# Loading both query weights in two pieces, of 16 and of 112 partitions

## The chip, the cores and the metric

The kernel runs on one core of a Trainium2 chip. The metric is the device time of one execution in microseconds. The core has a matrix engine (TensorE, PE in the profile), a vector engine (VectorE, DVE), an engine for functions (ScalarE, ACT), GpSimd (POOL) and SyncE (SP), which here only issues transfers. Transfers run on sixteen DMA engines and go from the chip's large memory into a memory of 128 partitions.

## The reference: two decode attentions and a gate

One token for each of two batch rows attends to two key and value caches, A and B. Both have 32 heads, 4096 positions and 128 values per head, in float32. The reference, cut to what matters:

```python
def attend(x, k_cache, v_cache, wq, wo):        # for A and for B
    q = (x @ wq).reshape(B, 1, 32, 128).transpose(0, 2, 1, 3)
    p = softmax(einsum("bhqd,bhkd->bhqk", q, k_cache) * 128 ** -0.5)
    o = einsum("bhqk,bhkd->bhqd", p, v_cache)
    return o.transpose(0, 2, 1, 3).reshape(B, 1, 4096) @ wo

g = sigmoid((x * gate_w).sum(-1, keepdims=True))
out = g * attend(x, A...) + (1 - g) * attend(x, B...)   # x is A_x for both
```

Each weight `wq` is 512 x 4096 values, 8 MB. Each cache is 134 MB, and there are four.

## The kernel before

**Units.** The work is cut into 32 units: cache A or B, a group of four heads, and one batch row. A unit has 8 MB of keys and 8 MB of values, each laid out as 128 partitions x 128 positions x 128 values, so that a partition holds 64 KB of it. Three buffers of this size exist: `kt[0]` and `kt[1]` take the keys in turn, and `vt` takes the values.

**The query weights.** They use `vt` too, before any value is loaded. `load_wq` copies a whole weight into `vt`: partition p gets rows 4p to 4p + 3 of the weight, 64 KB in one run. `projections` (lines 327 to 341) is a loop of two rounds on TensorE, one per weight: it waits on the semaphore `wq_landed`, takes its count off again, and multiplies x with the weight (L337). `queries` then scales the result on ScalarE (L348), into `vt` itself, and turns it on VectorE (L352, L353) into columns in `qcol`. Only then is `vt` free for the second weight, and after its turn for the values.

**The order of transfers.** SyncE issues nearly all transfers in program order, and each waits there until its buffer is free: the weight of A, the keys of unit 0 in two halves, the weight of B, the keys of unit 1, the values of unit 0, and from then on keys and values in turn, at the end the output weights `wo` of A and of B in pieces. The first two issues wait for nothing. The weight of B waits for the last reader of the first weight's result in `vt` (L353 on VectorE). `x` and the gate's weight come by ScalarE's queue, a few KB.

**The loops.** For each unit VectorE multiplies the keys in place with the spread query (L392) and sums (L395), which gives scores and frees the key buffer (`k_free`). It finds the maxima; ScalarE makes the exponentials (L367); TensorE multiplies them with the values (L371); ScalarE then frees `vt` (`v_free`). The keys of unit 0 are handled apart, in halves (L496, L498), between the two weights' queries. After the last unit come the sums, the output projection (L466, L481) and the two stores.

SyncE's own order at the beginning, in the program before (L220 is the load of a weight, L106 the keys of unit 0 in two halves, L231 keys, L239 values):

```order
L220 DMA vt<-in_A_wq_dram 128x16384
L106 DMA kt_85<-in_A_k_cache_dram 128x8192 x2
L106 UNCONDITIONAL_BRANCH
L220 DMA vt<-in_B_wq_dram 128x16384
L231 DMA kt_86<-in_A_k_cache_dram 128x16384
L239 DMA vt<-in_A_v_cache_dram 128x16384
```

The functions that the change touches, and what calls them:

Of the kernel before, what the change touches and what calls it, by code (L numbers as in the profile page):

```python
# [12 lines left out]
P = 128  # L13
# [10 lines left out]
KC = D // P  # L24
# [119 lines left out]
def tile_gated_decode(ctx: ExitStack, tc: tile.TileContext, ins: dict, out: bass.AP):  # L144
    nc = tc.nc
# [27 lines left out]
    vt = big.tile([P, NS, DH], F32, name="vt")  # L173
# [8 lines left out]
    with tc.tile_critical():  # L182
        S = Streams(nc, tc)
        put, take = S.put, S.take
# [13 lines left out]
        wq_landed, cleared, projected = sem("wq_landed"), sem("cleared"), sem("projected")  # L198
# [18 lines left out]

        def load_wq(n):
            S.before("sp", [], [r_vt])
            nc.sync.dma_start(vt.rearrange("p r d -> p (r d)"),  # L220
                              ins[n + "_wq"].rearrange("(p c) f -> p (c f)", c=KC)).then_inc(wq_landed, 16)

        def load_k(u):
            if u == 0:
# [33 lines left out]
        class Scratch:  # L258
# [3 lines left out]
            def take(self, n):  # L262
                self.at += -(-n // 128) * 128
                return self.t[:, self.at - -(-n // 128) * 128:][:, :n]
# [5 lines left out]
        def vput(e, make, reads=(), writes=(), **kw):  # L270
# [5 lines left out]
        r_kt[1].readers.append(S.dma("act", rows[B:B + 1], ins["gate_w"].rearrange("(o d) -> o d", o=1), writes=[r_gatew],  # L276
                                     slot="y"))
        load_wq("A")
        load_k(0)

# [46 lines left out]
        def projections():  # L327
            S.wait("pe", r_cols.writers)
            with nc.Fori(0, 2, engines=[mybir.EngineType.PE]):
                take("pe", wq_landed, 16)  # L330
                take("pe", cleared)
                blocks = vt.rearrange("p r d -> p (r d)").rearrange(
                    "p (c i g h d) -> p c i h g d", c=KC, i=NG // STRIPS, h=G, d=DH)
                for c in range(KC):
                    for i, t in enumerate(qa):
                        for h in range(G):
                            last = nc.tensor.matmul(t[h * QT:h * QT + B], cols[:, c],  # L337
                                                    blocks[:, c, i, h], start=c == 0, stop=c == KC - 1)
                last.then_inc(projected, 1)
# [134 lines left out]
        def strips(*which):  # L474
            for s in which or range(STRIPS):
                yield s, r_acc[s], acc[s][s * QT:s * QT + B, :W], slice(s * W, (s + 1) * W)
# [5 lines left out]


        projections()
        queries("A")
        load_wq("B")
        load_k(1)
        blank_projection()
# [77 lines left out]
        for n in range(2):  # L566
            for b in range(B):
                c = n * B + b
# [22 lines left out]
        for h, e in enumerate(("sp", "act")):  # L591
            r_total = [R(), R()]
            for i in range(2):
                _, a, t, _ = next(strips(2 * h + i))
# [27 lines left out]
```

## Time and profile before

| | |
|---|---|
| median of 3 runs | 1324.02 us (1323.88 to 1324.05) |
| the profiled execution's own time | 1324.03 us |
| its span, first to last instruction | 1322.2 us |
| bytes read | 570.43 MB |
| busy share of the 16 DMA engines, queue of SyncE | 99.6% |
| busy share of VectorE, TensorE, ScalarE | 88%, 25%, 8% |
| first weight issued, second weight issued | 0.96 us, 35.66 us |
| from issue to landing, first weight, second weight | 21.8 us, 25.8 us |

A row of a timeline gives the start and the length in us, the engine, the line of the kernel, the operation, and what is written from what; "SPq" is SyncE issuing a transfer. A row of the DMA part gives a queue with its packets, the MB moved, and the share of sixteen engines' time that the packets took. "GB/s" rows cut a stretch into forty equal slices and count each packet where it starts.

### The profile page before, as it was taken

To read this page: it belongs to the slowest core of one execution; us is meant where nothing else is said; L and a number is where in the kernel's file an instruction comes from. 1 tells how busy PE (TensorE), PEld (TensorE's weight loads), DVE (VectorE), ACT (ScalarE), POOL (GpSimd) and SP (SyncE) were. 2 spreads that over 40 slices of the span, in tenths; PEclk is the share of its full clock that TensorE was granted. 3 is DMA by queue.
4 is the path that set the end of the run, shared out by engine and by line. 5 is a ranking of instruction groups with operands and counts; after the bars stand their busy time and mean duration, and the time that the engine had idled before them with its cause. 6 is when DMAs were issued, how large, how long until landed. Compare 5 with 4: busy or idle time off the path is not lost. (4 is left out here: it accounts for less than half of the span.)

```text
span 1322.2 us, 6170 instructions
## 1 busy us (share of the span) xinstructions
PE 333.5 (25%) x2358; PEld 90.2 (7%) x2358; DVE 1165.2 (88%) x316; ACT 100.7 (8%) x328; POOL 0.7 (0%) x6
## 2 busy tenths in 40 slices
PE   3112223211222221122222122222212232221255
PEld 0000000000000000000000000000000000000011
DVE  1988999999999999999999999999999999999961
ACT  0000100001010000101000010100001010000100
POOL 0000000000000000000000000000000000000000
PEclk9566666556666655666665566666556666655678
DMA  9999999999999999999999999999999999999998
GB/s 406 451 412 443 442 418 442 440 428 432 442 432 426 442 440 418 442 442 416 442 442 418 442 442 428 430 442 434 424 442 442 416 442 442 416 442 442 423 438 350
DMA packets 10820, 570.51 MB, mean 431 GB/s; under 512 B 1207, under 2 KB 1467, under 8 KB 1726
## 3 DMA queue, kind: packets, MB, share of 16 engines
q1 hardware_dynamic: 10804, 570.43, 99.6%
q8 instruction: 3, 0.05, 0.0%
q14 instruction: 3, 0.02, 0.0%
q10 hardware_dynamic: 10, 0.01, 0.0%
HBM read 570.43 MB, written 0.00 MB: 431 GB/s over the span
## 5 line engine op out<-in xcount | busy, mean ns | idle before, releaser
L392 DVE TENSOR_TENSOR kt<-kt,q 128x16384 f32<-128x16384 f32 x31 | 534.0, 17225 | 70.6 <-DVEq L97 70.6
L395 DVE TENSOR_REDUCE sc<-kt 128x128 f32<-128x16384 f32 x31 | 533.8, 17220 | 1.1
L371 PE MATMUL vp<-vt,pr 128*32 128x512 f32 x1984 | 285.0, 739 | 913.5 <-PEq L97 913.5
L371 PEld LDWEIGHTS vp<-vt,pr 128*32 128x32 f32 x1984 | 78.3, 133 | 1120.2 <-issue 1120.2
L367 ACT ACTIVATE pr<-sc,nm 32x128 f32<-32x128 f32 x128 | 50.9, 398 | 107.0 <-ACTq L97 101.7
L430 ACT ACTIVATE pr<-nil 128x512 f32<-128x512 f32 x31 | 19.3, 623 | 457.4 <-ACTq L97 457.4
L451 ACT ACTIVATE vs<-vp,slot 128x128 f32 x15 | 5.5, 367 | 448.6 <-ACTq L97 448.6
L337 PE MATMUL qa<-vt,cols 128*2 128x512 f32 x128 | 19.1, 764 | 39.3 <-PEq L97 39.3
L367 ACT ACTIVATION_READ_ACCUMULATOR pr<-sc,nm (+1 forms) x128 | 23.5, 184 | 0.0
L416 DVE SCALAR_TENSOR_TENSOR vs<-vp,slot,vs 128x128 f32 x45 | 15.8, 351 | 8.6 <-DVEq L97 7.6
L597 DVE COPY kt<-qa 2x128 f32<-2x128 f32 x1 | 0.3, 278 | 23.6 <-PE qa L481 23.6
L352 DVE STREAM_TRANSPOSE vt<-vt 128x1024 f32<-128x1024 f32 x2 | 2.5, 1225 | 17.2 <-ACT vt L348 17.2
L498 DVE TENSOR_REDUCE sc<-kt 128x64 f32<-128x8192 f32 x2 | 17.4, 8686 | 0.1
L496 DVE TENSOR_TENSOR kt<-kt,q 128x8192 f32<-128x8192 f32 x2 | 17.4, 8686 | 0.0
L455 ACT ACTIVATE vp<-nil 128x512 f32<-128x512 f32 x15 | 9.0, 600 | 98.5 <-ACTq L97 98.5
L544 DVE SCALAR_TENSOR_TENSOR vs<-vp,slot,vs 128x128 f32<-128x128 f32 x3 | 1.1, 351 | 13.4 <-ACT vs L542 13.3
L371 PE MATMUL vp<-kt,pr 128*32 128x512 f32 x64 | 9.5, 759 | 10.4 <-DMA kt<-in_B_v_cache_dram 10.4
L400 DVE TENSOR_REDUCE rm<-sc 128x1 f32<-128x128 f32 x31 | 8.7, 281 | 2.3
L406 DVE STREAM_TRANSPOSE q<-qsel 128x128 f32<-128x128 f32 x30 | 9.3, 311 | 1.0
L466 PE MATMUL most<-vt,kt 128*2 128x512 f32 x64 | 8.4, 684 | 6.0 <-DMA vt<-in_A_wo_dram 6.0
L289 DVE COPY cols<-bank 128x8 f32<-128x8 f32 x1 | 0.2, 166 | 10.2 <-PE bank L287 10.2
L401 DVE STREAM_TRANSPOSE across<-rm 128x32 f32<-128x32 f32 x31 | 6.6, 212 | 1.1
(73 smaller groups left out, 56.7 us busy)
## 6 DMA issues: line engine op xcount, KB each, us to landing
kt<-in_A_k_cache_dram SPq DMA_DIRECT2D x2, 4096.0 KB, 35.6
kt<-in_B_wo_dram SPq DMA_DIRECT2D x1, 4096.0 KB, 33.3
kt<-in_B_wo_dram SPq DMA_DIRECT2D x1, 2048.0 KB, 37.7
kt<-in_B_wo_dram SPq DMA_DIRECT2D x1, 1024.0 KB, 39.7
kt<-in_B_wo_dram SPq DMA_DIRECT2D x1, 512.0 KB, 40.5
vt<-in_A_v_cache_dram SPq DMA_DIRECT2D x16, 28.3
kt<-in_B_k_cache_dram SPq DMA_DIRECT2D x16, 42.6
kt<-in_B_wo_dram SPq DMA_DIRECT2D x1, 256.0 KB, 40.6
```

The source lines that it names most:

```text
L337: last = nc.tensor.matmul(t[h * QT:h * QT + B], cols[:, c], blocks[:, c, i, h], start=c == 0, stop=c == KC - 1)
L367: do(lambda x: x.activation(padded[h, :, b, j * VC:(j + 1) * VC], s[h].rearrange("p (c a) -> p c a", a=VC), AF.Exp, bias=m[h], accum_out=l ...
L371: return x.matmul(vp[c % STRIPS * QT:(c % STRIPS + 1) * QT], padded[:, c].rearrange("p b m -> p (b m)"), t[:, c * VC:(c + 1) * VC].rearran ...
L392: at = D_.do(lambda x: x.tensor_tensor(kt[o], kt[o], q[:, None, :].to_broadcast([P, NS, DH]), op=ALU.mult), after)
L395: at = D_.do(lambda x: x.tensor_reduce(sc[o], kt[o], axis=AX.X, op=ALU.add), at)
L400: at = D_.do(lambda x: x.tensor_reduce(rm, sc[o], axis=AX.X, op=ALU.max), after)
L406: return D_.do(lambda x: x.transpose(q, qsel[:, 0].to_broadcast([P, DH // QT, QT])), at)
L416: at = D_.do(lambda x: x.scalar_tensor_tensor(vs[:, g], vp[:, a * DH:(a + 1) * DH], slot[:, a:a + 1], vs[:, g], op0=ALU.mult, op1=ALU.add) ...
L430: return A_.do(lambda x: x.activation(padded[:, :, b], nil[:, :, None].to_broadcast([P, NVC, G * VC]), AF.Copy))
L455: A_.do(lambda x: x.activation(vp, nil.to_broadcast([P, VC * DH]), AF.Copy))
L496: put("dve", lambda x: x.tensor_tensor(t, t, q[:, None, :].to_broadcast([P, NS // 2, DH]), op=ALU.mult), [r_q], [r])
L498: put("dve", lambda x: x.tensor_reduce(sc[0][:, h * NS // 2:(h + 1) * NS // 2], t, axis=AX.X, op=ALU.add), [r], [R()])
```

## The change

`load_wq` issues two transfers in place of one: the first 16 partitions of `vt` from the first 16 of the weight's layout, and then the other 112. Both add 16 to the same semaphore `wq_landed`, and TensorE waits for 32 in place of 16 before each projection and takes 32 off. Bytes, layout and everything else stay as they are. Lines after 220 move down by one, so L337 becomes L338, L392 becomes L393, and so on.

```diff
         def load_wq(n):
             S.before("sp", [], [r_vt])
-            nc.sync.dma_start(vt.rearrange("p r d -> p (r d)"),
-                              ins[n + "_wq"].rearrange("(p c) f -> p (c f)", c=KC)).then_inc(wq_landed, 16)
+            t, src = vt.rearrange("p r d -> p (r d)"), ins[n + "_wq"].rearrange("(p c) f -> p (c f)", c=KC)
+            for i, j in ((0, P // 8), (P // 8, P)):
+                nc.sync.dma_start(t[i:j], src[i:j]).then_inc(wq_landed, 16)
 
         def load_k(u):
...
         def projections():
             S.wait("pe", r_cols.writers)
             with nc.Fori(0, 2, engines=[mybir.EngineType.PE]):
-                take("pe", wq_landed, 16)
+                take("pe", wq_landed, 32)
                 take("pe", cleared)
```

SyncE's order with the change, in the same place:

```order
L222 DMA vt<-in_A_wq_dram 16x16384
L222 DMA vt<-in_A_wq_dram 112x16384
L106 DMA kt_85<-in_A_k_cache_dram 128x8192 x2
L106 UNCONDITIONAL_BRANCH
L222 DMA vt<-in_B_wq_dram 16x16384
L222 DMA vt<-in_B_wq_dram 112x16384
L232 DMA kt_86<-in_A_k_cache_dram 128x16384
L240 DMA vt<-in_A_v_cache_dram 128x16384
```

Each of the two loads has become two rows; nothing else has moved.

## The prediction

> **What bounds the kernel now.** I read the page's first lines first, then the DMA view of the long middle stretch, then the chain of waits, and last the two places where the query weights are loaded.
>
> ```profile
> span 1322.2 us, 6170 instructions
> PE 333.5 (25%) x2358; PEld 90.2 (7%) x2358; DVE 1165.2 (88%) x316; ACT 100.7 (8%) x328; POOL 0.7 (0%) x6
> DMA  9999999999999999999999999999999999999998
> q1 hardware_dynamic: 10804, 570.43, 99.6%
> ```
>
> VectorE is busy for 88% of the span, but the sixteen DMA engines for 99.6%, all of it on q1, the queue that SyncE fills. The DMA view of the stretch from 100 to 1200 us says the same without start and end:
>
> ```profile
> DMA packets 8178, 477.13 MB, mean 434 GB/s; under 512 B 896, under 2 KB 896, under 8 KB 896
> q1 hardware_dynamic: 8176, 477.11, 100.1%
> ```
>
> The rate is 434 GB/s with no idle time (100.1% for packets counted by their start). The bytes at this rate are the time: 570.43 MB / 434 GB/s = 1314.4 us of a span of 1322.2 us. The rest is start and end. So a stretch in which the DMA engines move fewer bytes in a microsecond is paid at the end in full.
>
> VectorE follows at a short distance:
>
> ```profile
> L392 DVE TENSOR_TENSOR kt<-kt,q 128x16384 f32<-128x16384 f32 x31 | 534.0, 17225 | 70.6 <-DVEq L97 70.6
> L395 DVE TENSOR_REDUCE sc<-kt 128x128 f32<-128x16384 f32 x31 | 533.8, 17220 | 1.1
> SPq L239 <- ACTq L134: 1000.6, 30, 34.9
> ```
>
> A unit of work needs 17.2 + 17.2 us here and some 2 us of small operations, while its 16.78 MB of K and V need 38.7 us. VectorE waits 70.6 us over 31 units, 2.3 us in each; this is its slack. The third row is SyncE waiting to issue V loads: a transfer is still ahead of them then, so the rings don't run dry.
>
> Now the first weight, in the DMA view from 2 to 21 us, forty slices of 0.475 us (rates by the start of each packet):
>
> ```profile
> GB/s 1798 276 0 0 0 0 1518 690 0 0 0 1246 966 0 0 0 1242 966 0 0 0 828 1380 0 0 0 690 1518 0 0 0 414 1794 0 0 0 276 1932 0 0
> q1 hardware_dynamic: 127, 8.32, 104.2%
> ```
>
> 127 packets hold 8.32 MB, so a packet is 65.5 KB: one partition's whole row of the weight (4 x 4096 values of 4 bytes). They start in eight bursts five slices apart: sixteen engines take one row each, together, eight times. One **round** is 16 x 65,536 B / 434 GB/s = 2.416 us. The rounds keep step; no engine falls behind another. Everything below is counted in rounds.
>
> **The change part by part.** Each 128-row load becomes a load of 16 rows and a load of 112. No bytes are added and no instruction changes but one wait count. The instructions around the loads, from the queue's timeline and those of TensorE and VectorE, and the loads' times from issue to landing:
>
> ```profile
> 0.96 0.40 SPq L220 DMA_DIRECT2D vt<-in_A_wq_dram  x1
> 1.41 0.89 SPq L106 DMA_DIRECT2D kt<-in_A_k_cache_dram  x2
> 23.04 9.84 PE L337 MATMUL qa<-vt,cols 128*2 128x512 f32 x64 [10.42 <-PEq L97]
> 35.44 0.20 DVE L353 COPY qcol<-vt 128x64 f32<-128x64 f32 x1
> 35.66 0.33 SPq L220 DMA_DIRECT2D vt<-in_B_wq_dram  x1
> 36.19 0.33 SPq L231 DMA_DIRECT2D kt<-in_A_k_cache_dram  x1
> vt<-in_A_wq_dram SPq DMA_DIRECT2D x1, 21.8
> vt<-in_B_wq_dram SPq DMA_DIRECT2D x1, 25.8
> ```
>
> *The extra issue on SyncE*, 0.33 to 0.40 us per weight: at 0.96 us it delays the K issue behind it (1.41), whose data comes after eight rounds; at 35.66 us K of unit 0 is still on the rings. Cost 0, hidden by 19.3 us of transfer ahead; without that cover it would be 0.4 us each.
>
> *The wait count* (32 for 16): same instruction, same place. Behind it on TensorE are the 64 matmul records of L337; behind these ScalarE's copies, VectorE's transpose and copy (L353, 35.44), and the issue of the second weight 0.2 us after it. So a first weight that lands x later moves the second weight's issue by x. K of unit 0 sits ahead of it on the same rings and moves by x too, so their distance stays: the rings hold 16 rounds from about 2.0 us, to 40.7 us, and the second weight is issued at 35.66. These 4 to 5 us cover the issue and stay so on the slowest engine. Cost 0 beyond x.
>
> *The order of rows on the engines* is what can cost. In the 128-row form each engine carries 8 rows, and eight even rounds show that the rows in flight together don't get in each other's way. No trace here has a large transfer to fewer partitions, so I bound it. In a 16-row piece the sixteen engines all write neighbouring partitions at once.
>
> Term 1, the 16-row piece. Lower bound: each partition can be written at an engine's full speed beside its neighbours; one round, 2.4 us, as now, extra 0. Upper bound: the way into the memory that an engine now has to itself serves 8 neighbouring partitions; then 16 rows go in by two ways and take 8 rounds, 19.3 us, extra 7 rounds. The middle is 4.5 rounds; as the rows divide evenly only by 1, 2, 4 or 8, I take groups of four neighbours behind one way: 4 rounds, extra 3 rounds = 7.2 us.
>
> Term 2, the 112-row piece. I take it that each engine gets 7 rows in a run. The even case is 7 rounds, extra 0 (with term 1's own round, eight as now). If two engines share each way throughout, it takes 14 rounds, extra 7. [...] I take 2.5 rounds, 6.0 us. An engine's delay isn't given to another, since rows are bound to engines; the weight is complete, and later buffers come free, by the slowest.
>
> Sum: 5.5 rounds x 2.416 = 13.3 us per weight, 26.6 us for both. The profiled execution took 1324.03 us, 1.8 us more than its span, and the median of the runs is 1324.02; the sum is made against the first: 1324.03 + 26.6 = **1350.6 us**. None of it is hidden: VectorE's 2.3 us of slack per unit is room behind the DMA engines, which themselves have none. PE, ACT and VectorE only start later.
>
> [...]
>
> **The rivals.**
>
> *No sharing: no change.* Each partition takes a row at full speed whoever writes beside it, so 1 + 7 rounds replace 8. For it: the page shows 100.1% busy engines and even rounds, which fits engines that are limited by themselves alone. Against it: the same evenness is what one sees if the 128-row form was dealt out to avoid meetings. Time 1324.0, at most 0.8 us more if neither issue were covered. This is the side that is not slower; it decides when an engine's own speed, 65,536 B in 2.416 us, is below what a shared way gives it.
>
> *Deep sharing.* The 112 rows are dealt one by one, so that each round is again 16 neighbours. Then all 8 rounds take four: 32 in place of 8, 24 x 2.416 = 58.0 us per weight, 1324.03 + 116.0 = 1440.0 us. For it: nothing in the trace says how rows are dealt. Against it: engines out of step would spread over other partitions.
>
> *An earlier start.* The first round begins about 1.0 us after the issue at 0.96; a small first piece might start sooner. If all of that went, once (the second weight meets full rings): 1324.03 - 1.0 = 1323.0 us. Too small to count as faster.
>
> **How the numbers follow.** Sharing at term 1 and part of term 2: 0.69. Its own range goes from term 1 alone, 2 x 7.2 = 14.5, 1338.5 us, to a weight that takes twice its time, 8 extra rounds, 2 x 19.3 = 38.7, 1362.7 us. Deep sharing 0.08, no sharing 0.19, an earlier start 0.04. A measurement of this kernel tells about 0.2%, 2.65 us, from no change. The two small cases lie inside that band; I leave 0.02 of them to more than it on the fast side. So slower 0.77, same 0.21, faster 0.02. To leave no more than 2 in 10 outside, the range takes in the two small cases, from 1323.0, and the main case with a little above its end, to 1366.0; deep sharing stays out. I put sharing well above no sharing because the one cost is bounded by 0 on the good side, and the bad side has many ways to come about.
>
> **What would show it.** Right: the first weight's bursts come unevenly, the first 16 rows take more than one round (about 10 us), the first matmul of L337's successor starts near 36 us instead of 23.04, the second weight is issued near 49 us, lands after more than 35 us instead of 25.8, and from the third transfer on the rate is 434 GB/s with everything some 27 us later. Term 1 alone: the first matmul near 30 us. No sharing: bursts five slices apart as before and the first matmul at 23 us. Wrong altogether: a delay before the second weight's issue that the first weight's landing doesn't explain, or lost time in the K and V stretch, at over 38.7 us a unit.

## The result: 45.5 us slower, 3.4%

The kernel with both weights in two pieces takes 1369.42 us (median of 6 runs, 1368.39 to 1370.69); the kernel before took 1323.92 us in the same comparison. The ratio is 1.0343, with a 95% interval of 1.0333 to 1.0353. The forecast was 1350.6 us in a range up to 1366.0. The sign was right, and so was the kind of cost, a lower rate while the weights are loaded. The size was not, because one step of the sum took it that engines don't hold each other up.

The page of the changed kernel, its DMA part over the whole span:

```profile
span 1367.8 us, 6172 instructions
...
DMA  9999999999999999999999999999999999999997
GB/s 215 305 240 418 432 435 430 431 429 433 441 437 433 431 431 431 431 445 435 433 431 429 433 441 437 435 431 429 433 441 435 437 429 431 433 433 443 435 430 321
...
q1 hardware_dynamic: 10836, 570.43, 99.5%
...
L393 DVE TENSOR_TENSOR kt<-kt,q 128x16384 f32<-128x16384 f32 x31 | 534.0, 17225 | 71.0 <-DVEq L97 71.0
```

The same row of the kernel before:

```profile
GB/s 406 451 412 443 442 418 442 440 428 432 442 432 426 442 440 418 442 442 416 442 442 418 442 442 428 430 442 434 424 442 442 416 442 442 416 442 442 423 438 350
```

The bytes are the same (570.43 MB) and the DMA engines are as busy as before (99.5% against 99.6%). Nearly all of the loss stands in the first three slices, of 34.2 us each (33.1 before): 215, 305 and 240 GB/s, where the kernel before had 406, 451 and 412. A busy DMA engine is not one that moves its bytes at full rate. From the fourth slice to the last but one the rate lies between 418 and 445 GB/s, before between 416 and 443, and VectorE waits in its loop as long as before (71.0 us against 70.6). The DMA view of a stretch of 1100 us in the middle confirms it, 434 GB/s as before:

```profile
DMA packets 8198, 477.46 MB, mean 434 GB/s; under 512 B 911, under 2 KB 911, under 8 KB 911
...
q1 hardware_dynamic: 8196, 477.43, 100.2%
```

The timeline of the beginning:

```profile
0.96 0.85 SPq L222 DMA_DIRECT2D vt<-in_A_wq_dram  x2
...
44.86 8.38 PE L338 MATMUL qa<-vt,cols 128*2 128x512 f32 x64 [30.06 <-PEq L97]
...
55.80 0.20 DVE L354 COPY qcol<-vt 128x64 f32<-128x64 f32 x1
56.02 0.79 SPq L222 DMA_DIRECT2D vt<-in_B_wq_dram  x2
...
108.58 8.95 PE L338 MATMUL qa<-vt,cols 128*2 128x512 f32 x64 [55.34 <-PEq L97]
```

The same view of the kernel before has the second projection here:

```profile
61.73 9.27 PE L337 MATMUL qa<-vt,cols 128*2 128x512 f32 x64 [28.86 <-PEq L97]
```

The first projection starts at 44.86 us in place of 23.04, 21.8 us later. The second weight is issued 20.4 us later than before. Its projection starts at 108.58 us in place of 61.73, so it is 46.8 us late, 25.0 of them new. The landing times of the changed kernel, each the median over the two pieces of a weight, and that of K of unit 0 behind the first weight (35.6 us before):

```profile
kt<-in_A_k_cache_dram SPq DMA_DIRECT2D x2, 4096.0 KB, 60.1
...
vt<-in_A_wq_dram SPq DMA_DIRECT2D x2, 27.8
vt<-in_B_wq_dram SPq DMA_DIRECT2D x2, 36.4
```

The weight of A landed in 21.8 us before; a median of 27.8 over a small and a large piece says little, but K, whose own transfers are as before, is 24.5 us later in the median of its two halves. The first half lands after 52.3 us in place of 31.0: what is queued behind a slow transfer is late with it. The second lands after 67.9 us in place of 40.2, since its last rows also meet the second weight (see e3). At the end of the kernel the loss is 45.5 us. The rest of the document asks why each weight costs over 20 us and not 13.3.

The packets of a trace have a start and a length. Put in order and taken sixteen at a time, the first 128 of them are the eight steps in which the engines take a weight's rows. This is the median length in each step, in us, for the first weight, from the trace of each kernel (in the kernel before, the first step holds some 0.7 us of starting up):

```
step of 16 rows of 64 KB        1     2     3     4     5     6     7     8
before, 128 partitions       3.10  2.42  2.42  2.42  2.42  2.42  2.42  2.42
the change, 16 + 112         8.59  5.38  4.71  2.98  3.82  4.45  4.66  4.43
e2, 0-63 + 64-127            4.64  5.13  5.13  5.13  4.91  5.13  5.13  5.13
e4, eight neighbouring 16s   8.59  9.34  9.39  9.39  9.40  9.39  9.40  9.40
e5, 32-95 + 0-31 + 96-127    3.05  2.42  2.42  2.42  4.56  5.13  4.91  5.13
e6, eight 16s, eight apart   4.76  5.12  5.11  5.11  4.90  5.12  5.12  5.12
e7, 16 + seven 16s           8.64  5.19  4.79  2.90  3.58  4.45  4.69  4.45
e8, 112 + 16                 4.04  4.76  4.79  3.69  3.50  4.64  4.78  8.31
```

### The profile page after: what moved, and what is told of

It reads as the page before. It is cut to its first block, busy times and chain, and to the rows that moved or that the text cites. A ratio compares the mean times of both kernels' runs of the same rounds, so it can differ in the third digit from the quotient of the medians.

```text
span 1367.8 us, 6172 instructions
## 1 busy us (share of the span) xinstructions
PE 333.0 (24%) x2358; PEld 90.2 (7%) x2358; DVE 1165.3 (85%) x316; ACT 100.6 (7%) x328; POOL 0.7 (0%) x6
## 3 DMA queue, kind: packets, MB, share of 16 engines
q1 hardware_dynamic: 10836, 570.43, 99.5%
HBM read 570.43 MB, written 0.00 MB: 417 GB/s over the span
## 5 line engine op out<-in xcount | busy, mean ns | idle before, releaser
L393 DVE TENSOR_TENSOR kt<-kt,q 128x16384 f32<-128x16384 f32 x31 | 534.0, 17225 | 71.0 <-DVEq L97 71.0
L338 PE MATMUL qa<-vt,cols 128*2 128x512 f32 x128 | 17.3, 702 | 85.4 <-PEq L97 85.4
L338 PEld LDWEIGHTS qa<-vt,cols 128*2 128x2 f32 x128 | 3.3, 94 | 98.6 <-issue 98.6
```

The costliest lines, as they stand in the source:

```text
L338: last = nc.tensor.matmul(t[h * QT:h * QT + B], cols[:, c], blocks[:, c, i, h], start=c == 0, stop=c == KC - 1)
L393: at = D_.do(lambda x: x.tensor_tensor(kt[o], kt[o], q[:, None, :].to_broadcast([P, NS, DH]), op=ALU.mult), after)
```

## The experiments

In all of them a weight is loaded whole, and TensorE waits for as many landings as there are pieces. The diffs are against the changed kernel, but for the last three; those of e4 to e8 are cut to the line that chooses the pieces.

### e1: two pieces of all 128 partitions

```diff
-            for i, j in ((0, P // 8), (P // 8, P)):
-                nc.sync.dma_start(t[i:j], src[i:j]).then_inc(wq_landed, 16)
+            for at in (slice(0, KC * H * DH // 2), slice(KC * H * DH // 2, KC * H * DH)):
+                nc.sync.dma_start(t[:, at], src[:, at]).then_inc(wq_landed, 16)
```

> Each weight in two pieces again, but of all 128 partitions and half of each partition's row (32 KB). Theory S (what costs is which partitions are written at once, through a limited number of ways): no change, 1323.9 us within 0.2%, rows of 32 KB at 1.21 us each. Rival P (every further piece costs by itself, some 22 us a weight, whatever it holds): 1369 us.

Measured: 1324.03 us, ratio 1.000 (0.999 to 1.001). The timeline of TensorE:

```profile
22.93 9.30 PE L338 MATMUL qa<-vt,cols 128*2 128x512 f32 x64 [12.67 <-PEq L97]
...
61.64 8.72 PE L338 MATMUL qa<-vt,cols 128*2 128x512 f32 x64 [29.42 <-PEq L97]
```

Both projections start where they did before (23.04, 61.73). A second transfer costs nothing that can be measured here; the second issue and the second count on the semaphore are covered, as the prediction had it. Rival P falls.

### e2: two halves, 0 to 63 and 64 to 127

```diff
-            for i, j in ((0, P // 8), (P // 8, P)):
-                nc.sync.dma_start(t[i:j], src[i:j]).then_inc(wq_landed, 16)
+            for at in (slice(0, P // 2), slice(P // 2, P)):
+                nc.sync.dma_start(t[at], src[at]).then_inc(wq_landed, 16)
```

> Each weight in two pieces of 64 partitions, 0 to 63 and 64 to 127. Theory S with sixteen engines taking runs of four neighbouring rows and eight ways reached per piece: two rows share a way all the time, 16 rounds in place of 8 per weight, 2 x 19.3 us more, 1362.6 us, every row of 64 KB near 4.8 us. If the rows were dealt one by one (16 neighbours at a time): four share, rows near 9.7 us, 1439.9 us. Rival P: 1369 us as with 16 and 112, since there are two pieces here too. Rival G (only groups of four neighbours share, each with a way of its own): no change.

Measured: 1366.66 us, ratio 1.032 (1.030 to 1.034). The time alone is close to both S and P, but P is gone with e1, and the rows decide: 5.13 us in nearly every step, 2.12 times 2.42 us. That is the length that S expected of two rows that share all the time (near 4.8 us). It is neither the 9.7 us expected of rows dealt one by one nor the 2.42 us of rival G. Which two rows share, the trace doesn't show.

### e3: the first weight alone in two pieces

```diff
-            for i, j in ((0, P // 8), (P // 8, P)):
+            for i, j in ((0, P // 8), (P // 8, P)) if n == "A" else ((0, P),):
                 nc.sync.dma_start(t[i:j], src[i:j]).then_inc(wq_landed, 16)
+            if n == "B":
+                nc.sync.sem_inc(wq_landed, 16)
```

> Only the first weight in pieces of 16 and 112, the second in one. If the two costs are independent: half of 45.5 us, 1346.7 us. If the second weight's cost came from the first one's aftermath: more than 1360 or under 1335 us.

For the weight of B, SyncE adds the second 16 itself, so that TensorE's wait for 32 stays.

Measured: 1344.73 us, ratio 1.0156 (1.0136 to 1.0177): 20.7 us for the first weight, which leaves 24.8 us for the second. The costs add up nearly evenly. The second is somewhat dearer; in the trace of the change fourteen of its first sixteen rows start from 61.05 to 62.88 us and two only at 67.83 and 68.56, where the first weight's start within 0.8 us. Two rows of keys that start at 62.97 and 63.73 us, beside the first rows of the weight, take 4.9 and 4.8 us in place of 1.21, and end where these two begin. The two projections of e3:

```profile
45.30 8.42 PE L340 MATMUL qa<-vt,cols 128*2 128x512 f32 x64 [30.96 <-PEq L97]
...
83.89 9.60 PE L340 MATMUL qa<-vt,cols 128*2 128x512 f32 x64 [30.17 <-PEq L97]
```

They start 38.6 us apart, as before (23.04 and 61.73, 38.7): after the first weight nothing more is lost.

### e4: eight pieces of 16 neighbours

```diff
+            for at in [slice(16 * i, 16 * i + 16) for i in range(8)]:
```

> Each weight in eight pieces of 16 neighbouring partitions, so it is known which row an engine writes when. Theory S: every piece is a copy of the first piece of the change, which took 8 to 9 us for a row; eight of these are 64 to 72 us in place of 19.3, 1324 + 2 x 45 to 2 x 58: 1414 to 1440 us. Rival P at about 22 us for each further piece: 7 x 22 x 2 = 308 us more, 1632 us. A theory by which small pieces are only slow at the start: under 1380 us.

Measured: 1434.45 us, ratio 1.083 (1.081 to 1.086), inside what S expected. From the second step on every step takes 9.34 to 9.40 us, 3.88 times 2.42. The DMA view from 2 to 41 us, slices of 0.975 us, shows what that looks like:

```profile
GB/s 1008 0 0 0 0 0 0 0 403 674 0 0 0 0 0 0 0 269 202 605 0 0 0 0 0 0 0 336 739 0 0 0 0 0 0 0 134 336 605 0
DMA packets 145, 5.18 MB, mean 133 GB/s; under 512 B 65, under 2 KB 65, under 8 KB 66
```

Sixteen rows start together, and then none for seven slices. So sixteen neighbouring partitions take nearly the four rounds that term 1 of the prediction gave them. The bytes, the engines and the number of rows in flight are those of the kernel before; only which partitions are written at once differs, and with them the rows of the weight that are read at once.

### e5: 64 partitions across the middle

```diff
+            for at in (slice(32, 96), slice(0, 32), slice(96, P)):
```

> Each weight in three pieces: partitions 32 to 95, then 0 to 31, then 96 to 127. The first has 64 rows like the first piece of the run with two halves, but lies across the middle. [...] 4 + 2 x 2 x 2.1 rounds: about 12.4 in place of 8 per weight, 1323.9 + 2 x 10.6 = 1345 us. Rival N (a transfer to fewer than 128 partitions is slow by itself, two rows of 64 KB per 5 us, wherever it lies): 1366 us or more, all rows near 5.1 us.

Measured: 1345.71 us, ratio 1.0176 (1.0158 to 1.0194), where 1345 was expected. The same view of this kernel:

```profile
GB/s 941 134 0 1078 0 67 1008 0 1075 0 202 874 0 0 0 672 403 0 0 0 403 672 0 0 0 403 672 0 0 0 34 504 202 336 538 538 504 235 336 538
```

The first bursts follow each other by two to three slices, full rate; from the fifth on they are four to five apart. Partitions 32 to 95 take a row in 2.42 us, partitions 0 to 63 (e2) in 5.13, with 64 rows in four steps both times. So a narrow transfer isn't slow by itself, and rival N falls. The sum of the expectation, four rounds for the middle rows and 2.1 for each step of the two pieces of 32, was the author's estimate: that 32 to 95 would keep 2.42 us no earlier run shows. This trace does: 2.42 us from the second step to the fourth, and for the pieces of 32 4.56 us in the fifth step, 4.91 in the seventh and 5.13 in the sixth and the eighth.

In all these runs the rows that are read move with the partitions that are written, so no run separates the two ends of a transfer. But if 64 rows are dealt in runs of four, e2 and this run read rows at the same distances, four rows from engine to engine, so a cause that goes by the distance of the rows in the large memory would have made both alike.

### e6: sixteen partitions, eight apart

```diff
+            for at in [slice(i, P, 8) for i in range(8)]:
```

> Each weight in eight pieces of 16 partitions as in the run with eight neighbouring sixteens, but the 16 lie eight apart (0, 8, 16 and so on). Theory S: they reach eight ways, so two share and not four: rows near 5.1 us in place of 9.39, 8 x 5.13 = 41.0 in place of 19.3 us, 1323.9 + 2 x 21.7 = 1367 us. Rival N' (the number of rows in a piece decides): 1434 us as with neighbours. Rival E (a way serves eight neighbours): rows at 2.42 us, no change.

Measured: 1367.09 us, ratio 1.0326 (1.0305 to 1.0346). The DMA view from 2 to 41 us:

```profile
GB/s 1008 67 0 0 67 809 202 0 0 67 672 336 0 0 0 605 471 0 0 0 336 739 0 0 0 336 739 0 0 0 67 807 202 0 0 0 739 336 0 0
```

A burst every five slices, where e4 had one every nine to ten. Rows take 5.11 us where sixteen neighbours took 9.39, in pieces of the same size and number. Rivals N' and E fall. Of the theories put up here that leaves S, for whole steps of 5.1 and of 9.4 us. The eight ways of its expectation are an estimate of the author's; the rows show 5.11 us, 2.11 times 2.42. The second weight lies elsewhere in the large memory, and its steps from the second on agree with those of the first within 0.05 us in e2, e4 and e6.

### e7: the 112 rows in seven pieces of 16, seven apart

```diff
+            for at in [slice(0, 16), *(slice(16 + i, P, 7) for i in range(7))]:
```

> The 112 rows of the change are loaded in seven pieces of 16 that lie seven apart, behind the first piece of 16: each engine then writes the same rows in the same order as if the piece of 112 were dealt in runs of seven, and no transfer of 112 exists. Theory L (dealt in runs; in each step one or two ways are shared by two rows, and all sixteen engines go at their pace): as with the change, 1369 us, all rows of a step at 3 to 4.8 us. Theory F (dealt in runs, only the rows that share are slow): 1354 us, most rows at 2.42 us; then the 112 piece was dealt otherwise or costs by itself.

Measured: 1369.16 us, ratio 1.0341 (1.0321 to 1.0362), the time of the change to 0.3 us. The DMA view from 2 to 41 us of the changed kernel:

```profile
GB/s 1075 0 0 0 0 0 0 0 473 605 0 0 0 0 874 202 0 0 0 1075 0 0 941 0 134 0 874 67 134 0 471 403 202 0 0 538 403 134 0 101
DMA packets 153, 8.49 MB, mean 218 GB/s; under 512 B 21, under 2 KB 21, under 8 KB 22
```

and of this kernel:

```profile
GB/s 1010 0 0 0 0 0 0 67 336 674 0 0 0 67 1008 0 0 0 67 1008 0 0 941 0 134 134 807 0 134 67 672 202 134 0 67 739 134 134 0 202
DMA packets 256, 8.52 MB, mean 219 GB/s; under 512 B 121, under 2 KB 121, under 8 KB 123
```

The bursts lie in the same slices or beside them, and the eight steps in the table agree within 0.25 us. So the piece of 112 goes as if it were dealt in runs of seven neighbouring rows, as the prediction assumed, and 112 is no bad number by itself. The one or two shared ways of theory L, and the 1354 us of theory F, come from a count of the author's that no run shows. F's rows can be tested without it: most were to take 2.42 us. The table's medians are 4.4 to 5.4 us in five of the seven steps, and the shortest of the 112 rows of the first weight takes 2.75 us in both runs. In the third step of the change all sixteen rows take 4.69 to 4.88 us, longer than the 2.42 us of full rate and shorter than the 5.13 us of e2. Whole steps are slowed, and F falls.

### e8: the mirror, 112 and then 16

```diff
+            for at in (slice(0, 112), slice(112, P)):
```

> The mirror of the change: partitions 0 to 111 first, then the last 16. Theory L: again 7 steps with one or two shared ways and one step of four: as with the change, 1365 to 1372 us. [...]

Measured: 1367.67 us, ratio 1.033 (1.031 to 1.035). Theory L expected 1365 to 1372. No row of the first seven steps takes less than 3.02 us, so here too theory F, by which most rows were to keep 2.42 us (e7), doesn't fit. Steps 4 and 5 are again the quick ones, 3.69 and 3.50 us. That one or two ways are shared in each of the seven steps is L's assumption and not shown.

### e9, e10, e11: sixteen partitions, seven apart and five apart, in one step

These put one transfer of 16 partitions into the kernel before, behind the first weight, where the engines are in step: in e9 partitions seven apart from 18 on, in e10 seven apart from 0 on, in e11 five apart from 0 on.

```diff
         load_wq("A")
+        k1, cut = tokens("_k_cache", 1), NS // 8
+        at = slice(18, 124, 7)      # e10: slice(0, 106, 7); e11: slice(0, 76, 5)
+        r_kt[1].readers.append(S.dma("sp", kt[1][at, cut:], k1[at, cut:], slot="extra"))
         load_k(0)
```

> The kernel before, with one extra transfer behind the first weight: 16 partitions seven apart from 18 on, 57,344 B each (keys of unit 1, which are loaded again later), into the second key buffer. [...] Theory L (all engines go at the pace of the way that is shared): all 16 rows take near 4.3 us in place of 2.12, 1324.0 + 4.3 = 1328.3 us. [...]

> [...] Theory L: all rows near 4.3 us, 1328.3 us. [...]

> [...] Theory L: all rows near 4.3 us, as with two ways, 1328.3 us. [...]

Measured: 1327.63 us (ratio 1.0028, 1.0017 to 1.0038), 1328.10 us (1.0030, 1.0018 to 1.0041) and 1328.33 us (1.0031, 1.0019 to 1.0043). The times lie too close together to decide; the sixteen rows do (57,344 B each, 2.12 us at 2.42 us for 64 KB), in us from the traces:

```
                         shortest  median  longest
e9, seven apart from 18      2.20    2.21     4.44   (13 rows from 2.20 to 2.25)
e10, seven apart from 0      3.41    3.62     4.03
e11, five apart from 0       3.63    3.94     4.12
```

The profile shows the same in the single microsecond from 24 to 25 us, first e9, then e10:

```profile
DMA packets 30, 0.49 MB, mean 492 GB/s; under 512 B 15, under 2 KB 15, under 8 KB 15
```

```profile
DMA packets 0, 0.00 MB, mean 0 GB/s; under 512 B 0, under 2 KB 0, under 8 KB 0
```

In e9, fifteen engines have gone on to the keys by 25 us (fifteen small packets for the landing and fifteen rows). In e10 none has. So neither theory is whole. In e9 three rows are slow (2.62, 2.79 and 4.44 us), and the other thirteen nearly keep their 2.12 us, where L expected all sixteen near 4.3. In e10 all sixteen go at nearly the same pace, 3.41 to 4.03 us, and in e11 too, 3.63 to 4.12 us: no row is at the 2.12 us of theory F's rows that don't share, and none reaches L's 4.3 us. How many ways are shared in each of the three no run shows; the two ways named in the expectation of e11 are a count of the author's for e10. But e9 is not the whole of its sixteen partitions either. With the 112 rows dealt in runs of seven they are those of the fourth step of the change, and there every row was slowed: 2.75 to 4.61 us, with a median of 2.98, where 2.21 us for 57,344 B would be 2.53 for 64 KB.

## Why the prediction was wrong

**What bounds the kernel, and that a lower rate is paid in full: right.** The DMA engines stay at 99.5%, the middle runs at 434 GB/s, and what the two weights lose comes out at the end: 46.8 us by the second projection, 45.5 us in the total.

**The parts costed at nothing: right.** e1 has the same extra issue and the same wait for 32, and takes 1324.03 us.

**The second weight moves with the first: right.** It was forecast for "near 49 us" and was issued at 56.02, 11.2 us after the first projection's start as against 12.6 before; nothing else delayed it.

**Term 1: right.** "I take groups of four neighbours behind one way: 4 rounds, extra 3 rounds = 7.2 us." e4 measures it apart from the start: 9.39 us in place of 2.42, 7.0 us extra. Within the change the first step took 8.59 in place of 3.10, 5.5 us. The four was chosen among 1, 2, 4 and 8 with no row of the trace behind it, so that its size came out is in part luck.

**Term 2: this step failed.** "I take 2.5 rounds, 6.0 us." From the end of the first step to the end of the eighth the seven steps take 32.0 us (11.64 to 43.59 in the trace), before 16.9 us (5.53 to 22.43): 15.1 us extra, 6.2 rounds. No run shows the 2.5; the runs showed 6.2 in its place. The runs of seven fit (e7). What was wrong is the sentence "An engine's delay isn't given to another, since rows are bound to engines". No run had shown it. It fits thirteen rows of e9, 2.20 to 2.25 us beside one of 4.44, but not the steps in which all sixteen rows are slowed to about the same length: 4.69 to 4.88 us in the third step of the change, 3.41 to 4.03 us in the single step of e10. By the prediction's own upper case, two rounds for each of the seven steps, a weight takes 4 + 7 x 2 = 18 rounds in place of 8, 48.3 us for both. Measured were 45.5. In the first weight the fourth and the fifth step, 2.98 and 3.82 us, are together 2.9 us below two rounds each; the other five lie from 0.4 us below it to 0.6 us above.

**The range.** Its upper end for the likeliest case, "a weight that takes twice its time", added 8 rounds, while the ends of the two terms, 7 and 7, allow 14. Measured were about 9 for the first weight (21.8 us) and 10 for the second (25.0). An end that the text had itself derived was left out of the range.

**The rivals.** No sharing falls by e4, deep sharing by e7 (the rows are dealt in runs) and by its 1440.0 us, the earlier start by the first packets, which begin at 2.00 us in place of 1.99.

**Open:** which partitions slow each other in a step, why all sixteen rows are slowed in e10, and why those of e9 are not when the same partitions were in the fourth step of the change. No run here looks behind the packets, and e9 to e11 are sixteen rows of one trace each. For all sixteen to be slow it doesn't take engines that are out of step: the rows of e10 start within 0.6 us of each other, those of the sixth step of the change within 2.1 us (27.59 to 29.67), and both are slow throughout. For the partitions of e9 it may matter what ran just before: steps of 2.42 us in e9, and in the change a step of 4.71. And since the rows that are read always moved with the partitions, no run excludes that the large memory has a part in it.

## What to carry to other kernels

Cut a large transfer along the row and not across the partitions: two pieces of 128 partitions cost nothing here (1324.03 us, e1), and two pieces of 16 and 112 cost 21 to 25 us for 8 MB. Where fewer partitions must be written, time the choice of them from a trace, since a row took 2.42 us in 32 to 95 and 5.13 us in 0 to 63. And when a term of a sum assumes that a delay stays with the engine that has it, put the case that it stops all of them into the range.

## What was not expected of the hardware

The slowing of all sixteen rows of a step together: 3.41 to 4.03 us in e10 and 3.63 to 4.12 us in e11, in a step by itself, where 2.12 us is the length at full rate. In e2's two halves a row takes 5.13 us, 2.12 times the 2.42 us of the load of 128 partitions and so a little more than twice; in e4's sixteen neighbours it takes 9.39 us, 3.88 times and so a little less than four times. And the share of time in which the DMA engines are busy stayed at 99.5% over the span while the rate fell to 215 GB/s in the first slice: the busy share says nothing of such a loss, and the GB/s row shows it at once.
